# GFNet spectral filter beside an S2-MLP block on one core: spectral chunks in other banks, inverse sums in own buffers, half sums moved, one more unit of seven products

## The chip, the cores and the metric

The kernel runs on one core of one Trainium2 chip. The metric is device time in microseconds (us) of one execution; less is better. The core's engines have queues of their own and meet at semaphores: PE (matrix products, with its weight loads shown as PEld), DVE (vector work), ACT (activations and copies), POOL (more vector work) and SP, whose queue issues the DMAs.

## The reference

The input `x` has 2048 tokens of 448 channels; F is 1792. What is computed, cut to its core:

```
xn = layernorm(x)
A  = irfft2(rfft2(xn) * (w_r + 1j * w_i))          # over tokens and channels
h  = gelu(layernorm(xn) @ w1)                      # 448 x 448
hs = shift(h, quarters by +1, -1, +2, -2 tokens) @ w2
x1 = xn + hs
B  = x1 + gelu(layernorm(x1) @ w3) @ w4            # 448 x 1792, 1792 x 448
out = x + A + B
```

## The kernel before

Every product is made in float16 with each operand split into a high and a low half, so that one product is three passes on the PE (`PASS`: high by high, high by low, low by high). ACT writes the high half of a result from its bank, DVE the low half.

The 2048 tokens are 16 blocks of 128. After the two norms and the products with w1 and w2 (lines L400 to L515) two strands of work run side by side on the PE:

- **The MLP** goes in groups `G` of 256 tokens (0 to 7) and units `fp` of 256 hidden columns (0 to 6). `front(G, fp)` makes 22 matmuls of 256 columns into a bank `pw3` (L400), ACT takes the GELU and the high half `hf`, DVE the low half (L726 to L729). `back(G, fp)` multiplies `hf` by w4 into two banks `acc`: 12 matmuls of 448 columns (L808). `ORD` lists the order of the units in a group.
- **Units of seven products.** For the units in `SEVEN[G]`, `back` runs `seven` instead (L778): the 2 x 2 blocks of a unit (two token blocks, two hidden blocks, w4 cut in two halves of columns) are multiplied in Strassen's manner with seven products in place of eight, so 21 matmuls of 224 columns into `acc` and two banks `side`. `sums` (L736 to L745) makes the sums of the hidden blocks, and `hz`. The sums of w4's blocks must be there before: `w4_sums(j, ...)` loads w4's rows of unit `j` again, makes four sums on DVE (L757) and splits them in a high half on ACT (L280) and a low half on DVE (L281). The sums for units 4, 5 and 0 are made in group 2 (tile `loads`), those for 1, 2 and 3 by `w4_late` at the units that the table `LATE` lists as `(j, G, fp)` (tile `late`).
- **The spectral strand.** After a transform along channels, 16 chunks `c` are worked on by `chunk_a` (`pp` on PE, then `pf` on ACT and DVE, L629 and L630), `chunk_b` (`px` on PE from `pf`, then `te` on ACT and twice on DVE, L644 to L646, and `z` on POOL, L648), `chunk_z` (`zb`, the halves of z, on ACT and DVE, L655 and L656) and `chunk_c` (`pu` on PE from `zb`, then `y` on ACT and DVE, L670 and L671). Each chunk needs its weights `wc` and two constant matrices `gn` by DMA. Then `gather_u` copies the result into `U` (eight DVE copies, L680, for half of the token blocks), `inv_a` makes `pe` on PE (L688), the tile `e` on ACT and DVE (L692 to L699) and `vh`, and `inv_b` makes `py` on PE (L709) and adds it to the output rows `xt`.

PSUM has eight banks, two for each of four tags: `mm`, `tr`, `sp` and `acc`. A new tile of a tag waits until the one two places before it has been read. Before the change `pp` and `pe` are in `tr`; `px`, `pu`, `py` and group 5's `side` are in `sp`. The temporary tiles `te`, `e` and `late` take two places `stage0` and `stage1` in turn.

No order is written out for the engines: a scheduler with a time model of its own merges the strands. MLP fronts and backs are the filler (`FILL`), what empties a bank goes first (`EVAC`), and `behind(key)` holds an instruction back in a queue until the instructions of that key have been placed.

Of the kernel before, what the change touches and what calls it, by code (L numbers as in the profile page):

```python
# [12 lines left out]
F32 = mybir.dt.float32  # L13
# [25 lines left out]
AFTER = [[], [3], [4], [5], [6], [7], [], []]  # L39
EVAC, FILL = 0, 100000  # L40
DH = D // 2
SEVEN = {5: [0, 4, 5], 6: [0, 4, 5, 1, 2, 3], 7: [0, 1, 2, 4, 5]}
ORD = {G: list(range(7)) for G in range(5)} | {5: [1, 2, 3, 6, 0, 4, 5], 6: [0, 4, 5, 1, 2, 3, 6],
                                               7: [0, 1, 2, 4, 5, 3, 6]}

ME = [0, 224] + list(range(2, 224, 2))
# [79 lines left out]
def body(tc, nc, x, wf, w1, w2, w3, w4, c_g, c_n, c_small, out):  # L126
# [14 lines left out]
    def pool(name, bufs=1, side="left", space=None):  # L141
        kw = dict(name=name, bufs=bufs, reuse_waits="tile")
        if space is not None:
            kw["space"] = space
        else:
            kw["side"] = side
        cm = tc.tile_pool(**kw)
        opened[name] = cm
        return cm.__enter__()
# [6 lines left out]
    def bank(tag, name):  # L156
        return ps.tile([128, 512], F32, tag=tag, bufs=2, name=name)

    pc = pool("pc")
    px = pool("px")  # L160
# [16 lines left out]
    def stage(name, n, side, dtype=F32):  # L177
        t = pw.tile([128, 1808], F32, tag=f"stage{side}", bufs=1, name=name)
        return (t if dtype is F32 else t.bitcast(dtype))[:, :n]
# [194 lines left out]
    @contextlib.contextmanager  # L374
    def behind(*key):
        key = key if len(key) > 1 else key[0]
        with contextlib.ExitStack() as st:
            for i in after[key]:
                st.enter_context(tc.issue_after(i))
            yield  # L380
# [202 lines left out]
    def w_scale_end():  # L583
        t = pc.tile([128, 4], F32, name="wt")
        V.tensor_reduce(out=t[:, 0:1], in_=wm, axis=AX.X, op=ALU.max)
        pt = bank("sp", "wpt")
        T.transpose(pt[0:1, 0:128], t[:, 0:1], ident)
        V.tensor_reduce(out=t[0:1, 1:2], in_=pt[0:1, 0:128], axis=AX.X, op=ALU.max)
        V.tensor_scalar(out=t[0:1, 1:2], in0=t[0:1, 1:2], scalar1=2.0 ** -20, scalar2=None, op0=ALU.max)
        pb = bank("sp", "wpb")  # L590
        T.matmul(pb[:, 0:1], ones[0:1], t[0:1, 1:2], start=True, stop=True)
        e = pc.tile([128, 3], I32, name="we")
        V.tensor_copy(out=t[:, 2:3], in_=pb[:, 0:1])
        V.tensor_single_scalar(e[:, 0:1], t.bitcast(I32)[:, 2:3], 0x7F800000, op=ALU.bitwise_and)
        V.tensor_single_scalar(e[:, 1:2], e[:, 0:1], 0x7F800000, op=ALU.bitwise_xor)
        V.tensor_scalar(out=sc[:, 0:1], in0=e.bitcast(F32)[:, 1:2], scalar1=ZPRE, scalar2=None, op0=ALU.mult)
        for h in range(2):
            V.tensor_scalar(out=sc[64 * h:64 * h + 64, 2:3], in0=sc[64 * h:64 * h + 64, 0:1], scalar1=2.0 * h - 1.0,
                            scalar2=None, op0=ALU.mult)
        V.tensor_scalar(out=sc[:, 1:2], in0=e.bitcast(F32)[:, 0:1], scalar1=2.0 ** -21 / (ZPRE * UPRE * VPRE),  # L600
                        scalar2=s12[:, 0:1], op0=ALU.mult, op1=ALU.mult)
        V.tensor_scalar(out=sc[:, 3:4], in0=sc[:, 1:2], scalar1=p12, scalar2=None, op0=ALU.mult)
# [30 lines left out]
    def chunk_b(c):  # L633
        w, k, _ = stream[c]
        pf = pfs.pop(c)
        px_ = bank("sp", f"px{c}")
        for h in range(2):
            for n, (pi, gi) in enumerate(PASS):
                T.matmul(px_[:, DF * h:DF * h + DF], k[:, gi, h], pf[:, pi, h], start=n == 0, stop=n == 2)  # L639
        src = px_[:, :2 * DF]  # L640
        o = stage(f"te{c}", 6 * DF, c % 2)
        e, t = o[:, :2 * DF], o[:, 2 * DF:].rearrange("p (a n) -> p a n", a=2)
        for h in range(2):
            A.activation(out=e[64 * h:64 * h + 64], in_=px_[64 - 64 * h:128 - 64 * h, :2 * DF], func=AF.Copy)  # L644
        V.scalar_tensor_tensor(out=t[:, 0], in0=src, scalar=sc[:, 0:1], in1=w[:, 0], op0=ALU.mult, op1=ALU.mult)
        V.scalar_tensor_tensor(out=t[:, 1], in0=e, scalar=sc[:, 2:3], in1=w[:, 1], op0=ALU.mult, op1=ALU.mult)  # L646
        z = pst.tile([128, 2 * DF], F32, tag="z", bufs=2, name=f"z{c}")
        P.tensor_tensor(out=z, in0=t[:, 0], in1=t[:, 1], op=ALU.add)  # L648
        zs[c] = z
# [8 lines left out]
    def chunk_c(c):  # L658
        _, _, k = stream.pop(c)
        zh = zb[c % 2]  # L660
        pu = bank("sp", f"pu{c}")
        for par in range(2):
            for h in range(2):
                d = pu[:, 256 * par:256 * par + 256].rearrange("p (q k) -> p q k", k=8)[:, :, 4 * h:4 * h + 4]
                for n, (zi, ki) in enumerate(PASS):
                    o = (2 * zi + h) * DF + 113 * par
                    T.matmul(d, zh[:, o:o + 128], k[:, ki, h].rearrange("p (q k) -> p q k", k=4), start=n == 0, stop=n == 2)  # L667
        src = pu[:113].rearrange("p (q n) -> p q n", q=4)
        d = [Y1[:113, p, :, c].rearrange("p q b k -> p q (b k)") for p in range(2)]
        A.activation(out=d[0], in_=src, func=AF.Copy, scale=UPRE)  # L670
        V.scalar_tensor_tensor(out=d[1], in0=src, scalar=UPRE, in1=d[0], op0=ALU.mult, op1=ALU.subtract)  # L671
# [11 lines left out]
    def inv_a(b):  # L683
        pe = bank("tr", f"pe{b}")
        for q in range(4):
            kd = 113 - q // 2
            for n, (ui, ii) in enumerate(PASS):
                T.matmul(pe[:, 113 * q:113 * q + 113], U[b // 8 * 8][ui][:kd, q, b % 8, :],  # L688
                         cI[ii][:kd, 113 * q:113 * q + 113], start=n == 0, stop=n == 2)
        w = stage(f"e{b}", 1126, b % 2)  # L690
        v, e = w[:, 452:900], w[:, 900:1126]
        A.activation(out=e, in_=pe[:, 226:452], func=AF.Copy)  # L692
        u = w[:, 0:452].rearrange("p (a b d) -> p a b d", a=2, b=2)
        uf = w[:, 0:452].rearrange("p (a n) -> p a n", a=2)
        V.tensor_tensor(out=uf[:, 0], in0=pe[:, 0:226], in1=e, op=ALU.add)
        V.tensor_tensor(out=uf[:, 1], in0=pe[:, 0:226], in1=e, op=ALU.subtract)
        va = v.rearrange("p (a d) -> p a d", a=2)
        V.tensor_tensor(out=va[:, :, 0:113], in0=u[:, :, 0], in1=u[:, :, 1], op=ALU.add)
        V.tensor_tensor(out=va[:, ::-1, 223:111:-1], in0=u[:, :, 0, 1:113], in1=u[:, :, 1, 1:113], op=ALU.subtract)  # L699
        vh = pv.tile([128, 2, D], F16, tag="vh", bufs=2, name=f"vh{b}")  # L700
        A.activation(out=vh[:, 0], in_=v, func=AF.Copy, scale=VPRE)
        V.scalar_tensor_tensor(out=vh[:, 1], in0=v, scalar=VPRE, in1=vh[:, 0], op0=ALU.mult, op1=ALU.subtract)
        vhs[b] = vh
# [45 lines left out]
    def w4_sums(j, part):  # L749

        t = part.rearrange("p (k n) -> p k n", n=DH)
        SY.dma_start(t.rearrange("p (f k) n -> p f (k n)", f=2), w4v[:, 2 * j:2 * j + 2])

        def go():
            for o, i, k, op in ((3, 3, 1, ALU.subtract), (1, 1, 0, ALU.subtract),
                                (0, 3, 0, ALU.add), (2, 2, 0, ALU.subtract)):
                V.tensor_tensor(out=t[:, o], in0=t[:, i], in1=t[:, k], op=op)  # L757
            split_w(w4t[j][:, 0], w4t[j][:, 1], t, s4)
        return go
# [60 lines left out]
    def mlp(Gs, hook=None, ahead=1, tags=("mm",)):  # L820
        with prio(FILL):
            todo = [(G, fp) for G in Gs for fp in ORD[G]]
            done = 0
            for n, (G, fp) in enumerate(todo):
                while done < min(n + 1 + (ahead if todo[n] != (7, 5) else 1), len(todo)):
                    front(*todo[done], tags[done % len(tags)])
                    if hook:
                        with prio(EVAC):
                            hook(*todo[done])
                    done += 1  # L830
                back(G, fp)
# [57 lines left out]
    n = 2  # L889
# [148 lines left out]
    close("pfd")  # L1038
    with behind("m", 2, 3):
        w_scale_end()  # L1040
    pst = pool("pst", side="right")
    zb = [pst.tile([128, 4 * DF + 16], F16, name=f"zb{i}") for i in range(2)]
    for i in range(2):
# [10 lines left out]
            chunk_c(i - 3)  # L1054
    close("pst")
    mlp(range(3, 5))
    pv = pool("pv", side="right")
    bs = [*range(8), *range(12, 16), *range(8, 12)]
    for n in range(17):
# [8 lines left out]
                finish(b)  # L1068
    close("pa2")
    pz = pool("pz")  # L1070
    LATE = [(1, 5, 0), (2, 5, 5), (3, 6, 4)]

    def w4_late(G, fp):
        for n, (j, *at) in enumerate(LATE):
# [33 lines left out]
```

## Time and profile before

| | |
|---|---|
| median of 3 runs | 408.02 us (407.68 to 408.14) |
| the profiled execution's own time | 408.05 us |
| its span, first to last instruction | 406.3 us |
| mean granted PE clock | 0.998 |
| PE busy | 399.9 us, 3391 matmuls |
| DVE busy | 333.6 us |
| ACT busy | 255.1 us |
| POOL busy | 100.4 us |

The profile is of one execution. Its page lists each engine's busy time, the span in 40 slices, the DMA queues, the chain of work that ended last, and groups of instructions with count, busy time, mean duration and the idle time ahead of them. Rows of the timeline hold start, duration, engine, line and tile; matmuls are pipelined, so that their pace is read from start to start and not from their durations. Tile names in the profile have no buffer numbers.

### The profile page before, as it was taken

How to read it: one execution, taken by the hardware profiler on the slowest of the kernel's cores; microseconds unless marked ns; L12 is line 12 of the kernel's file. 1: busy time of each engine (PE TensorE's matmuls, PEld its weight loads, DVE VectorE, ACT ScalarE, POOL GpSimd, SP SyncE). 2: the span in 40 equal slices, each digit the busy share in tenths (PEclk: the TensorE clock that was granted, in tenths of full speed). 3: DMA queues.
4: the chain of work that ended last, by engine and by line, in shares of the span. 5: the costliest groups of instructions: out<-in, count | busy, mean ns of one | idle time of the engine just before them, and what ended most of it. 6: DMA issues, size and time to landing. Idle time of an engine off the chain costs nothing.

```text
span 406.3 us, 8732 instructions
## 1 busy us (share of the span) xinstructions
PE 399.9 (98%) x3391; PEld 297.2 (73%) x3391; DVE 333.6 (82%) x702; ACT 255.1 (63%) x433; POOL 100.4 (25%) x158
## 2 busy tenths in 40 slices
PE   8999999999999999999999999999999999999996
PEld 3555555865667877777878878777677779998995
DVE  5898799898947887988698888965999999965645
ACT  4788889874568857655698878853354544353431
POOL 6859910111146946500021111110000000000000
PEclk9999999999999999999999999999999999999999
DMA  8978975567489661637256556510011023100101
GB/s 280 389 272 160 249 152 138 122 121 163 95 225 266 234 191 46 219 95 185 72 144 164 162 142 161 139 27 2 24 69 70 24 90 92 47 2 2 45 2 45
DMA packets 54596, 52.07 MB, mean 128 GB/s; under 512 B 35678, under 2 KB 48542, under 8 KB 54556
## 3 DMA queue, kind: packets, MB, share of 16 engines
q1 hardware_dynamic: 54556, 51.53, 46.0%
q8 instruction: 26, 0.43, 0.4%
q14 instruction: 14, 0.11, 0.1%
HBM read 38.28 MB, written 3.67 MB: 103 GB/s over the span
## 4 chain that ended last, share of the span: by engine, by line
PE 87%; POOL 5%; DMA 2%; DVE 2%; ACT 2%; issue 1%; SPq 0%; POOLq 0%; ACTq 0%
PE pw L400 33%; PE acc L808 23%; PE pw L478 6%; PE side L778 4%; PE acc L778 3%; PE pu L667 3%; PE ps L567 3%; PE pe L688 2%; PE pp L622 2%; PE px L639 2%; PE py L709 2%; PE pw L420 2%; DMA w1s<-w 1%; POOL xt L336 1%; DMA h<-x2mem 1%
## 5 line engine op out<-in xcount | busy, mean ns | idle before, releaser
L400 PE MATMUL pw<-x2mem,w3p 128*128 128x256 f16 x1232 | 151.3, 273 | 0.0
L400 PEld LDWEIGHTS <-w3p 128*128 128x128 f16 x1232 | 118.9, 98 | 19.3
L808 PE MATMUL acc<-w4p,hf 128*128 128x448 f16 (+1 forms) x516 | 104.4, 348 | 0.0
L808 PEld LDWEIGHTS <-hf 128*128 128x128 f16 x516 | 50.1, 98 | 37.6
L726 ACT ACTIVATE pw<-pw,pe 128x512 f32<-128x512 f32 x42 | 27.4, 654 | 26.8 <-PE pw L400 26.6
L729 DVE SCALAR_TENSOR_TENSOR hf<-pw,h,hf 128x512 f16<-128x512 f32 x42 | 31.3, 746 | 12.9 <-ACT hf L728 12.7
L478 PE MATMUL pw<-w2p,h 128*128 128x448 f16 x176 | 35.8, 353 | 0.9 <-DMA h<-x2mem 0.9
L420 PE MATMUL pw<-w1p,xT 128*128 128x448 f16 x176 | 34.9, 352 | 0.1
L648 POOL TENSOR_TENSOR z<-te 128x450 f32<-128x450 f32 x16 | 15.7, 983 | 70.8 <-DVE te L646 65.9
L728 ACT ACTIVATE hf<-pw,h 128x512 f16<-128x512 f32 x42 | 28.9, 687 | 5.0 <-PE acc L808 4.0
L478 PEld LDWEIGHTS <-h 128*128 128x128 f16 x176 | 17.0, 98 | 17.0 <-DMA h<-x2mem 2.0
L744 ACT ACTIVATE hz<-g,h 128x896 f16<-128x896 f32 x14 | 14.6, 1044 | 23.1 <-DVE g L741 23.1
L420 PEld LDWEIGHTS <-xT 128*128 128x128 f16 x176 | 17.1, 99 | 16.1 <-DVE xT L394 0.4
L778 PEld LDWEIGHTS <-hz 128*128 128x128 f16 x294 | 28.3, 98 | 0.6
L629 ACT ACTIVATE pf<-pp 64x450 f16<-64x450 f32 x32 | 17.4, 544 | 12.5 <-DVE pf L630 9.7
L630 DVE TENSOR_TENSOR pf<-pp,pf 64x450 f16<-64x450 f32 x32 | 19.9, 622 | 5.1 <-ACT pf L629 4.7
L745 DVE SCALAR_TENSOR_TENSOR hz<-g,h,hz 128x896 f16<-128x896 f32 x14 | 16.1, 1148 | 6.8 <-ACT hz L744 6.8
L550 POOL TENSOR_TENSOR f<-xr 128x452 f32<-128x452 f32 x16 | 19.7, 1251 | 0.6
L558 DVE TENSOR_TENSOR xh<-f,xh 128x452 f16<-128x452 f32 x16 | 14.3, 916 | 5.7 <-ACT xh L557 5.7
L644 ACT ACTIVATE te<-px 64x450 f32<-64x450 f32 x32 | 17.3, 541 | 1.2 <-PE px L639 0.6
L738 ACT ACTIVATE g<-pw,pe 128x512 f32<-128x512 f32 x14 | 9.6, 683 | 11.3 <-PE pw L400 11.3
L547 POOL TENSOR_TENSOR xr<-xf 128x452 f32<-128x452 f32 x8 | 9.2, 1156 | 22.3 <-issue 16.4
(188 smaller groups left out, 705.7 us busy)
## 6 DMA issues: line engine op xcount, KB each, us to landing
wc<-wf SPq DMA_DIRECT2D x32, 225.0 KB, 3.7
wl<-wf SPq DMA_DIRECT2D x8, 450.0 KB, 4.3
xt<-x SPq DMA_DIRECT2D x8, 448.0 KB, 7.1
xf<-x SPq DMA_DIRECT2D x8, 448.0 KB, 4.6
loads<-x SPq DMA_DIRECT2D x7, 448.0 KB, 4.0
out<-xt SPq DMA_DIRECT2D x13, 224.0 KB, 1.9
w3raw<-w SPq DMA_DIRECT2D x3, 896.0 KB, 10.8
gn<-c_g SPq DMA_DIRECT2D x16, 128.0 KB, 3.0
```

Source lines behind the costliest of these rows:

```text
L400: T.matmul(ps_out, wp[:, wi + t, cols], xT[:, xi + t, tok], start=t == 0 and wi + xi == 0, stop=t == 3 and wi == 4)
L420: m = T.matmul(pm[:, :D], xTs[g][:, xi + t, 128 * i:128 * i + 128], w1p[:, wi + t], start=t == 0 and p == 0, stop=t == 3 and p == 2)
L478: T.matmul(pm[:, :D], h[:, k], w2p[:, w], start=n == 0, stop=n == 10)
L550: P.tensor_tensor(out=f[:, :, k:k + 2].rearrange("p b s d -> p s b d"), in0=u[:, :, 0], in1=u[:, :, 1], op=op)
L629: A.activation(out=hi, in_=src, func=AF.Copy)
L630: V.tensor_tensor(out=lo, in0=src, in1=hi, op=ALU.subtract)
L644: A.activation(out=e[64 * h:64 * h + 64], in_=px_[64 - 64 * h:128 - 64 * h, :2 * DF], func=AF.Copy)
L726: A.activation(out=pm, in_=pm, func=AF.Gelu_apprx_tanh, scale=r3)
L728: i = A.activation(out=h[:, 0], in_=pm, func=AF.Copy, scale=h3)
L729: j = V.scalar_tensor_tensor(out=h[:, 1], in0=pm, scalar=h3, in1=h[:, 0], op0=ALU.mult, op1=ALU.subtract)
L778: m = T.matmul(to, h[:, hi, 128 * blk:128 * blk + 128], b[wi], start=new and n == 0, stop=n == 2 and (last if blk in (2, 5, 3, 0) else end ...
L808: m = T.matmul(to, h[:, hi, o:o + 128], w4p[0][:, wi, f, r], start=first and f % 2 == 0 and n == 0, stop=end and f % 2 == 1 and n == 2, sk ...
```

## The change

1. `px` and `pu` of chunks 14 and 15 take banks of the tag `tr` instead of `sp`.
2. The tile `e` of `inv_a` gets three buffers of its own in the pool `pv`.
3. The half sums of w4 for units 1 and 2 are made in group 4, behind units 0 and 2, from two tiles `early` of a new pool; `LATE` holds only unit 3, now at group 6's first unit.
4. Unit 1 of group 5 becomes a fourth unit of seven products there, and is the group's last in `ORD`.

```diff
-SEVEN = {5: [0, 4, 5], 6: [0, 4, 5, 1, 2, 3], 7: [0, 1, 2, 4, 5]}
-ORD = {G: list(range(7)) for G in range(5)} | {5: [1, 2, 3, 6, 0, 4, 5], 6: [0, 4, 5, 1, 2, 3, 6],
+SEVEN = {5: [0, 4, 5, 1], 6: [0, 4, 5, 1, 2, 3], 7: [0, 1, 2, 4, 5]}
+ORD = {G: list(range(7)) for G in range(5)} | {5: [2, 3, 6, 0, 4, 5, 1], 6: [0, 4, 5, 1, 2, 3, 6],
...
-        px_ = bank("sp", f"px{c}")
+        px_ = bank("tr" if c in (14,15,) else "sp", f"px{c}")
...
-        pu = bank("sp", f"pu{c}")
+        pu = bank("tr" if c in (14,15,) else "sp", f"pu{c}")
...
-        w = stage(f"e{b}", 1126, b % 2)
+        w = pv.tile([128, 1126], F32, tag="e", bufs=3, name=f"e{b}")
...
+    pt = pool("pt")
     pst = pool("pst", side="right")
...
     mlp(range(3, 5))
+    for n, j in enumerate((1,2,)):
+        with behind(("f", 4, 2 * n + 0)):
+            w4_sums(j, pt.tile([128, 896], F32, tag="early", bufs=2, name=f"early{j}"))()
+    close("pt")
     pv = pool("pv", side="right")
...
-    LATE = [(1, 5, 0), (2, 5, 5), (3, 6, 4)]
+    LATE = [(3,6,0)]
```

The order of instructions changes from the last chunks on. The first place is on the DVE, after the low half of group 4's first unit (`hf40`); `pf15` is what px15 reads, `pu10` and `px13` are banks of chunks 10 and 13. Before:

```order
L630 TENSOR_TENSOR pf14_3285<-pp14_3272,pf14_3285 64x2x225
L656 TENSOR_TENSOR zb0_2540<-z12_3248,zb0_2540 128x450
L671 SCALAR_TENSOR_TENSOR y1_1548<-pu10_3250,y1_1548 113x4x128
L645 SCALAR_TENSOR_TENSOR te13_3299<-px13_3292,sc_138,wc13_3209 128x450
L646 SCALAR_TENSOR_TENSOR te13_3299<-te13_3299,sc_138,wc13_3209 128x450
L630 TENSOR_TENSOR pf15_3341<-pp15_3328,pf15_3341 64x450
L729 SCALAR_TENSOR_TENSOR hf41_3769<-pw3_41_3745,h3_666,hf41_3769 128x512
L630 TENSOR_TENSOR pf15_3341<-pp15_3328,pf15_3341 64x2x225
```

After, at the same place:

```order
L757 TENSOR_TENSOR early1_3998<-early1_3998 128x224
L630 TENSOR_TENSOR pf14_3288<-pp14_3275,pf14_3288 64x2x225
L656 TENSOR_TENSOR zb0_2543<-z12_3251,zb0_2543 128x450
L671 SCALAR_TENSOR_TENSOR y1_1548<-pu10_3253,y1_1548 113x4x128
L757 TENSOR_TENSOR early1_3998<-early1_3998 128x224
L645 SCALAR_TENSOR_TENSOR te13_3302<-px13_3295,sc_138,wc13_3212 128x450
L646 SCALAR_TENSOR_TENSOR te13_3302<-te13_3302,sc_138,wc13_3212 128x450
L630 TENSOR_TENSOR pf15_3344<-pp15_3331,pf15_3344 64x450
L757 TENSOR_TENSOR early1_3998<-early1_3998 128x224
L729 SCALAR_TENSOR_TENSOR hf41_3772<-pw3_41_3748,h3_666,hf41_3772 128x512
L757 TENSOR_TENSOR early1_3998<-early1_3998 128x224
L630 TENSOR_TENSOR pf15_3344<-pp15_3331,pf15_3344 64x2x225
```

The four sums of early1 stand among the same instructions, all four ahead of the second part of pf15. Behind it follow, after the change, the two te of chunk 14, the low half of early1, zb of chunk 13, y of chunks 11 and 12 and zb of chunk 14.

The second place is on the PE, from px14 to the w4 unit of `hf41`; equal matmuls that follow each other, and weight loads, are left out. Before, px14 comes after 7 matmuls of pw3_42 and the 12 of pu11, and then:

```order
L639 MATMUL px14_3348<-pf14_3285,gn0_14_3268 128x225
...
L400 MATMUL pw3_42_3786<-x2mem_119,w3p_132 128x256
...
L808 MATMUL acc40_3772<-w4p_991,hf41_3769 128x448
...
L400 MATMUL pw3_43_3825<-x2mem_119,w3p_132 128x256
...
L667 MATMUL pu12_3362<-gn1_12_3158,zb0_2540 128x32x4
...
L639 MATMUL px15_3379<-pf15_3341,gn0_15_3324 128x225
```

After, px14 is the first thing behind the w4 unit of `hf40`:

```order
L639 MATMUL px14_3351<-pf14_3288,gn0_14_3271 128x225
...
L400 MATMUL pw3_42_3789<-x2mem_119,w3p_132 128x256
...
L667 MATMUL pu11_3309<-gn1_11_3105,zb1_2544 128x32x4
...
L667 MATMUL pu12_3365<-gn1_12_3161,zb0_2543 128x32x4
...
L639 MATMUL px15_3382<-pf15_3344,gn0_15_3327 128x225
...
L808 MATMUL acc40_3775<-w4p_991,hf41_3772 128x448
```

px15 has moved ahead of the w4 unit of `hf41` (12 matmuls): between px14 and px15 there are now 3 matmuls of pw3_42, 12 of pu11, 12 of pu12 and 14 of pw3_42, and behind px15 5 of pw3_42 and that unit. Then come 7 of pw3_43, 2 of pu14, 12 of pu13 and 10 of pu14, 15 of pw3_43, a w4 unit, and pu15 among the matmuls of pw3_44. The first `pe` has 7 matmuls of pw3_45 ahead of it where it had 2 of pw3_46 before.

The third place is SP's queue, as the difference; `y_1300` to `y_1407` are rows for the MLP's input, `early` and `late` w4's rows, `gn_15` the last chunk's second constant:

```order
 L514 DMA_TRANSPOSE x2mem<-y_1300 128x7x128 x2
 L514 DMA_TRANSPOSE x2mem<-y_1303 128x7x128 x2
+L752 DMA early_3998<-w 128x2x448
+L752 DMA early_4006<-w 128x2x448
 L514 DMA_TRANSPOSE x2mem<-y_1404 128x7x128 x2
 L514 DMA_TRANSPOSE x2mem<-y_1407 128x7x128 x2
...
+L614 DMA gn_14_3273<-c_n 128x512
+L752 DMA late_4852<-w 128x2x448
+L614 DMA gn_15_3329<-c_n 128x512
```

The two early loads have moved up to the MLP's input transposes of the second stage, and late3 stands ahead of the last load of a chunk, where three late loads stood among the output's DMAs.

## The prediction

> **What bounds the kernel now.** I read the page's first part, then the waits of the PE, then the chain that ended last and the PE's rows in order of time.
>
> ```profile
> span 406.3 us, 8732 instructions
> PE 399.9 (98%) x3391; PEld 297.2 (73%) x3391; DVE 333.6 (82%) x702; ACT 255.1 (63%) x433; POOL 100.4 (25%) x158
> PE wps L838 <- DVE wsrc L192: 1.2, 1, 1.2
> PE pw L478 <- DMA h<-x2mem: 0.9, 3, 0.4
> PE pta L389 <- POOL xt L336: 0.7, 1, 0.7
> PE pm L260 <- DVE pt L258: 0.4, 1, 0.4
> 347.62 1.15 PE side L778 x12
> 374.10 2.27 PE acc L808 x12
> 376.37 2.40 PE pw L400 x22
> ```
>
> The PE is busy 98% of the span. Its four listed waits sum to 3.2 us, and all stand at lines of the first, second and norm stages, which the change does not touch. From the first GELU product on, the PE goes from matmul to matmul. The last three rows give the pace: 2.27/12 = 189 ns for 448 columns, 1.15/12 = 96 ns for 224, 2.40/22 = 109 ns for 256. So the time is the sum of PE work plus whatever new wait appears, and an edit can gain only by taking columns off the PE.
>
> ```profile
> 257.00 2.43 PE L808 MATMUL acc<-w4p,hf 128*128 128x448 f16 x12
> 259.27 0.93 PE L400 MATMUL pw<-x2mem,w3p 128*128 128x256 f16 x7
> 260.03 0.83 PE L667 MATMUL pu<-gn,zb 128*128 128x128 f16 x12
> 260.70 0.74 PE L639 MATMUL px<-pf,gn 128*128 128x225 f16 x6
> 261.28 1.80 PE L400 MATMUL pw<-x2mem,w3p 128*128 128x256 f16 x15
> ...
> 266.40 0.74 PE L639 MATMUL px<-pf,gn 128*128 128x225 f16 x6
> ...
> 257.00:270.00 13.00, 13.00 (x113) 9.75 (x111) 10.69 (x17) 10.49 (x19) 1.96 (x2) 1.00 0.35 93
> 270.00:285.00 15.00, 15.00 (x147) 11.62 (x146) 7.93 (x18) 5.97 (x11) 0.98 (x1) 1.00 0.04 10
> 285.00:340.00 55.00, 55.00 (x511) 41.79 (x509) 53.10 (x125) 25.56 (x49) 0.00 (x0) 1.00 0.17 60
> ```
>
> From start to start, 12 pu matmuls take 0.67 us (56 ns each) and 6 px matmuls 0.58 us (97 ns each). In the stage rows (length, then busy PE, PEld, DVE, ACT, POOL), the DVE is free for 2.3 us of 13, then 7.1 us of 15, and then almost never: 53.1 of 55 us during the inverse transform. The PE is full in all three.
>
> **The change, part by part.** *Seven products for unit 1 of group 5.* Twelve matmuls of 448 columns go (12 x 189 = 2.27 us) and 21 of 224 come (21 x 96 = 2.02 us): **-0.25 us** on the PE, which is on the path.
>
> A rule of the Trainium skill speaks against this term: its page "TensorE: Matmul & The Clock Gate", section "Back-to-back issue gap", gives about 81 ns per matmul at 128 columns and 131 ns at 512 for a stream of weight loads and matmuls. On a straight line between these an estimate is 123 ns at 448 and 93 ns at 224, so twelve become 1.47 us, 21 become 1.96 us, and the term would be +0.49 us. The rows above (189 and 96 ns) do not agree with it, and the measurement decides.
>
> ```profile
> L745 DVE SCALAR_TENSOR_TENSOR hz<-g,h,hz 128x896 f16<-128x896 f32 x14 | 16.1, 1148 | 6.8 <-ACT hz L744 6.8
> L741 DVE TENSOR_TENSOR g<-g 128x384 f32<-128x384 f32 x14 | 7.8, 555 | 0.2
> L740 DVE TENSOR_TENSOR g<-g 128x256 f32<-128x256 f32 x14 | 5.9, 421 | 5.4 <-ACT g L738 5.4
> L729 DVE SCALAR_TENSOR_TENSOR hf<-pw,h,hf 128x512 f16<-128x512 f32 x14 | 10.5, 747 | 5.4 <-ACT hf L728 5.4
> L757 DVE TENSOR_TENSOR late<-late 128x224 f32<-128x224 f32 x12 | 4.7, 390 | 0.6 <-DMA late<-w 0.4
> L281 DVE SCALAR_TENSOR_TENSOR x2mem<-late,pe,x2mem 128x896 f16<-128x896 f32 x3 | 3.4, 1146 | 0.0
> L280 ACT ACTIVATE x2mem<-late,pe 128x896 f16<-128x896 f32 x3 | 3.1, 1028 | 0.0
> 340.00:360.00 20.00, 20.00 (x197) 18.86 (x196) 18.84 (x33) 9.10 (x11) 0.00 (x0) 1.00 0.14 47
> ```
>
> On the DVE the seven-product unit costs 421 + 555 + 1148 - 747 ns = 1.38 us more. It stands where two sets of half sums stood, each 4 x 390 + 1146 ns = 2.7 us, and these have gone from there, so the DVE is lighter by 5.4 - 1.4 = 4.0 us in the stretch to 360 us. I cost it at nothing. The set for unit 3 moves ahead by some units inside group 6, into that freed time: nothing.
>
> *The half sums for units 1 and 2 in group 4.* The same 5.4 us of DVE and 2 x 1028 ns of ACT now stand from 257 us on, ahead of spectral work that the PE reads. The windows have 9.4 us of free DVE time between 257 and 285 us, but not evenly spread.
>
> *Banks.* Chunks 14 and 15 take the first product's banks. In the new order the PE reaches px14 right after the first w4 unit of group 4, and px15 after px14, 3 pw, 24 pu and 14 pw matmuls. From the start of the second row above that is 259.27 + 0.58 + 0.33 + 1.34 + 1.53 = **263.05 us**, where before px15 starts at 266.40. px15 needs the second half of pf15.
>
> ```profile
> 256.99 0.63 DVE L630 TENSOR_TENSOR pf<-pp,pf 64x450 f16<-64x450 f32 x1
> 257.66 0.63 DVE L656 TENSOR_TENSOR zb<-z,zb 128x450 f16<-128x450 f32 x1
> 258.32 0.69 DVE L671 SCALAR_TENSOR_TENSOR y<-pu,y 113x512 f16<-113x512 f32 x1
> 258.93 0.68 DVE L645 SCALAR_TENSOR_TENSOR te<-px,sc,wc 128x450 f32<-128x450 f32 x1
> 259.52 0.68 DVE L646 SCALAR_TENSOR_TENSOR te<-te,sc,wc 128x450 f32<-128x450 f32 x1
> 261.42 0.63 DVE L630 TENSOR_TENSOR pf<-pp,pf 64x450 f16<-64x450 f32 x1
> 263.71 0.69 DVE L645 SCALAR_TENSOR_TENSOR te<-px,sc,wc 128x450 f32<-128x450 f32 x1 [0.28 <-ACT te L644]
> 279.23 2.77 DVE L680 COPY U<-y 113x1024 f16<-113x1024 f16 x8
> 282.68 0.36 PE L688 MATMUL pe<-csm,U 113*128 113x113 f16 x4
> ```
>
> The second pf15 ends at 262.05 us. The four subtractions and additions on early1 stand ahead of it now. The te rows show that the next instruction starts 0.09 us before the last ends, so four cost between 4 x 0.30 = 1.2 and 4 x 0.39 = 1.56 us, and pf15 ends between 263.25 and 263.61. The PE waits 0.2 to 0.56 us; I take **+0.35**, the value nearer to a running queue. Behind that wait on the PE's queue stand the rest of pw3_42 and the w4 unit, so all of it is paid.
>
> Next is pu14. After pf15 (263.4) the DVE has two te (0.6 each), the early1 low half (1.06), a zb and two y (0.6 each) and then zb of chunk 14: it ends at about 268.1. The PE, from px15 at 263.4, has 6 px, 5 pw, 12 w4, 7 pw, 2 and 12 pu matmuls: 263.4 + 0.58 + 0.55 + 2.27 + 0.76 + 0.11 + 0.67 = 268.3. That is covered by 0.2 us: taken at nothing, bounded by 0.5.
>
> Then the U copies. Ahead of pe0 the PE now has one w4 unit (2.27 us) and 17 pw matmuls (1.85) less, so it arrives at 282.68 - 4.1 + 0.35 = 278.9 us. The DVE's list from 256.99 to the last copy is 8 sums x 0.30, 2 low halves x 1.06, 19 operations of pf, zb, y and te x 0.6, three hf x 0.66 (0.75 less the overlap) and the copies, 2.77: 2.4 + 2.1 + 11.4 + 2.0 + 2.8 = 20.7 us, ending at 277.7 if it never waits, against the PE's need at 278.9 (first halves) to 279.3 (second halves). I expect about 0.7 us of waits on ACT and POOL in it, so no stall, bounded by 1.5 us.
>
> From there DVE and PE both run the inverse stage about 4 us sooner, with one hf (0.75 us) less on the DVE; its 1.9 free us of 55 leave room for small waits. I add **+0.1** there, between 0 and 0.8.
>
> *Own e buffers.* Three buffers in place of two shared ones take away waits of ACT and DVE only; the PE waited for none of them: nothing.
>
> *Loads.*
>
> ```profile
> 92.54 5.42 SPq L514 DMA_TRANSPOSE x2mem<-y  x4
> 104.78 5.24 SPq L514 DMA_TRANSPOSE x2mem<-y  x4
> late<-w SPq DMA_DIRECT2D x3, 448.0 KB, 3.5
> 265.13 0.98 POOL L648 TENSOR_TENSOR z<-te 128x450 f32<-128x450 f32 x1 [3.81 <-DVE te L646]
> gn<-c_n SPq DMA_DIRECT2D x16, 128.0 KB, 3.3
> ```
>
> The two early loads are issued between the transposes at 92.5 and 104.8, where SP has nothing from 97.96 on; their wait is for a matmul of the first product, which the h transposes ahead of them on SP need as well. With 3.5 us to landing they are in by about 103: nothing. late3 now stands on SP ahead of the last c_n load and waits for z14, which ends near 266 us; that load waits anyway for pu13, at about 268.3. Landing 3.3 us later it is in at 271.7, and pu15 comes 15 pw, 12 w4 and one pw after pu14, at about 272.8: covered by 1.1 us.
>
> **Sum.** -0.25 + 0.35 + 0.1 = +0.2 us on the profiled execution's 408.05 us (span 406.3 and 1.75 around it). The median of the runs, 408.02, is 0.03 below that, so both give **408.2 us**. About 0.2%, 0.8 us, is what a measurement of this kernel can tell from no change.
>
> **Rivals.**
> 1. *All waits are covered.* If the four sums slip into gaps, or pf15 is done by 263.05, only the PE term is left: 407.8 us. For it: the PE has no wait in these stages now. Against: the DVE is gapless from 256.99 to 263.4 in the rows. Chance 0.20.
> 2. *Slower: the DVE becomes the bound ahead of the inverse stage.* The copies of U end after the PE gets to pe0. The stall begins once the DVE's waits between 257 and 278 us sum to about 1.4 us, and it decides from about 2.0 on. For it: such waits are there now (0.28 us ahead of te alone), and the early low halves wait for ACT, with zb and y queued behind. Against: the list itself needs only 20.7 us. With 2.5 to 3.3 us of waits pe0 stalls 1.1 to 1.9 us; with the other terms that gives 409.3 to 410.1, in the middle 409.7. Chance 0.21.
> 3. *The seven products do not shorten the PE's work.* By the page's spacing the term is +0.49 in place of -0.25, so 408.9 us. The rows for 224 and 448 columns speak against it. Chance 0.01.
> 4. *Faster by over 0.8 us.* The change takes 0.25 us off the PE and no stage has a PE wait to give back, so this needs something that the profile does not show. Time 407.0. Chance 0.04.
>
> **How the numbers follow.** The forecast (stalls of 0.1 to 0.95 us in all, 407.9 to 408.7) gets 0.54. Same is 0.54 + 0.20 = 0.74, slower 0.21 + 0.01 = 0.22, faster 0.04. The range goes from 407.6 (rival 1 less 0.2 us, about half the spread of the runs, 407.68 to 408.14) to 409.5, which leaves out the faster case and about half of rival 2.
>
> **What would show it.** In the profile after: PE rows with 21 matmuls of L778 more and 12 of L808 fewer; a wait of px on the DVE's pf of 0.2 to 0.6 us near 263 us; pe starting near 278.9 us; no PE wait on U, te or vh over 0.3 us. A PE wait on U copies of 1 us or more, or several on vh in the inverse stage, makes it wrong towards rival 2; no PE wait at all makes it rival 1.

## The result, and the profile after

The changed kernel takes 409.06 us (median of 9 runs, 408.86 to 409.34), the kernel before 408.02 (9 runs, 407.62 to 408.38). The ratio is 1.0028 (95%: 1.0018 to 1.0038): slower by 0.28%, 1.04 us. That lies inside the range, but above the band of the forecast (407.9 to 408.7) and below that of rival 2 (409.3 to 410.1). "Same" had 0.74, and by the 0.8 us that the prediction set for it, it was not the same.

The first part of the page, two of the waits of the PE, and the PE's group of w4 products, of the kernel after:

```profile
span 407.3 us, 8758 instructions
PE 400.3 (98%) x3400; PEld 298.2 (73%) x3400; DVE 336.2 (83%) x704; ACT 255.4 (63%) x433; POOL 100.6 (25%) x158
PE px L639 <- DVE pf L630: 0.8, 1, 0.8
PE pu L667 <- DVE zb L656: 0.2, 1, 0.2
L808 PE MATMUL acc<-w4p,hf 128*128 128x448 f16 (+1 forms) x504 | 102.0, 348 | 0.0
```

The PE has 9 matmuls more (21 - 12), and two waits that it did not have. To see the change apart from the stages ahead of it, whose waits differ from run to run, I use the *products' part*: from the start of the first matmul of L808 to the end of the PE's last row. In the PE's timeline of the kernel before it is 401.32 + 1.69 - 87.39 = 315.62 us:

```profile
87.39 0.54 PE L808 MATMUL acc<-w4p,hf 128*128 128x448 f16 x2
401.32 1.69 PE L808 MATMUL acc<-w4p,hf 128*128 128x448 f16 x14
```

and in that of the kernel after 401.26 + 2.73 - 87.33 = 316.66 us, so all of the 1.04 us is in it:

```profile
87.33 0.54 PE L808 MATMUL acc<-w4p,hf 128*128 128x448 f16 x2
...
261.74 1.36 PE L400 MATMUL pw<-x2mem,w3p 128*128 128x256 f16 x11
263.86 0.74 PE L639 MATMUL px<-pf,gn 128*128 128x225 f16 x6 [0.75 <-DVE pf L630]
...
268.01 0.94 PE L667 MATMUL pu<-gn,zb 128*128 128x128 f16 x14
269.20 0.73 PE L667 MATMUL pu<-gn,zb 128*128 128x128 f16 x10 [0.24 <-DVE zb L656]
...
279.02 0.93 PE L400 MATMUL pw<-x2mem,w3p 128*128 128x256 f16 x7
279.78 0.36 PE L688 MATMUL pe<-csm,U 113*128 113x113 f16 x4
401.26 2.73 PE L808 MATMUL acc<-w4p,hf 128*128 128x224 f16 x21
```

Read from start to start, as in the prediction: 11 matmuls of 109 ns from 261.74 bring the PE to px15 at 262.94, and it starts at 263.86, 0.92 us late. 14 of 56 ns from 268.01 bring it to the rest of pu14 at 268.79, and it starts at 269.20, 0.41 us late. (The bracket and the waits list give less, since a row's modelled end runs past the next start.) I call such lateness a *loss*. -0.25 + 0.92 + 0.41 = +1.08 us, against +1.04 measured. The first pe comes 7 x 109 ns after 279.02, without a loss.

What delayed pf15 and zb of chunk 14 stands in the timelines of POOL and of the DVE:

```profile
260.83 1.01 POOL L648 TENSOR_TENSOR z<-te 128x450 f32<-128x450 f32 x1 [5.22 <-DVE te L646]
265.17 1.76 POOL L648 TENSOR_TENSOR z<-te 128x450 f32<-128x450 f32 x1 [3.33 <-ACT y L670]
```

```profile
260.61 0.61 DVE L630 TENSOR_TENSOR pf<-pp,pf 64x450 f16<-64x450 f32 x1
261.14 0.95 DVE L757 TENSOR_TENSOR early<-early 128x224 f32<-128x224 f32 x1
262.01 0.73 DVE L729 SCALAR_TENSOR_TENSOR hf<-pw,h,hf 128x512 f16<-128x512 f32 x1
262.68 0.37 DVE L757 TENSOR_TENSOR early<-early 128x224 f32<-128x224 f32 x1
263.08 0.63 DVE L630 TENSOR_TENSOR pf<-pp,pf 64x450 f16<-64x450 f32 x1
...
264.94 1.15 DVE L281 SCALAR_TENSOR_TENSOR x2mem<-early,pe,x2mem 128x896 f16<-128x896 f32 x1
266.00 1.41 DVE L656 TENSOR_TENSOR zb<-z,zb 128x450 f16<-128x450 f32 x1
268.53 0.61 DVE L656 TENSOR_TENSOR zb<-z,zb 128x450 f16<-128x450 f32 x1
```

The third sum of early1 takes 0.95 us where the fourth takes 0.37, and it ends at 262.09, 0.25 us after POOL's add of z13 (261.84). zb of chunk 13 takes 1.41 us where that of chunk 14 takes 0.61, and ends at 267.41, 0.48 us after POOL's add of z14 (266.93). That add itself took 1.76 us in place of 0.98: it began while the DVE's low half of early1 ran, and ended 0.84 us after it. The long DVE rows and POOL's add read all their inputs from SBUF. The sum costs 0.57 us on the way to px15, zb 0.78 on the way to pu14.

My theory: the two losses are the DVE's queue ahead of pf15, as forecast, plus a mutual blocking of the DVE and POOL (each holds the other up while it reads SBUF), which was not forecast. The rivals: the queue's length alone; the early sums as such, wherever the PE stands; the banks alone.

### The profile page after: what moved, and what is told of

It reads as the page before. It is cut to its first block, busy times and chain, and to the rows that moved or that the text cites. A ratio compares the mean times of both kernels' runs of the same rounds, so it can differ in the third digit from the quotient of the medians.

```text
span 407.3 us, 8758 instructions
## 1 busy us (share of the span) xinstructions
PE 400.3 (98%) x3400; PEld 298.2 (73%) x3400; DVE 336.2 (83%) x704; ACT 255.4 (63%) x433; POOL 100.6 (25%) x158
## 4 chain that ended last, share of the span: by engine, by line
PE 83%; DVE 5%; POOL 5%; ACT 3%; issue 2%; DMA 1%; DVEq 0%; POOLq 0%
PE pw L400 31%; PE acc L808 21%; PE pw L478 6%; PE side L778 4%; PE acc L778 3%; PE ps L567 3%; PE pe L688 2%; PE py L709 2%; PE wps L838 2%; PE pp L622 2%; PE pw L420 2%; PE pu L667 2%; PE px L639 2%; POOL xt L336 1%; DMA h<-x2mem 1%
## 5 line engine op out<-in xcount | busy, mean ns | idle before, releaser
L808 PE MATMUL acc<-w4p,hf 128*128 128x448 f16 (+1 forms) x504 | 102.0, 348 | 0.0
L808 PEld LDWEIGHTS <-hf 128*128 128x128 f16 x504 | 48.9, 98 | 36.6
L729 DVE SCALAR_TENSOR_TENSOR hf<-pw,h,hf 128x512 f16<-128x512 f32 x41 | 30.4, 743 | 11.8 <-ACT hf L728 11.4
L778 PEld LDWEIGHTS <-hz 128*128 128x128 f16 x315 | 30.3, 98 | 0.9
L744 ACT ACTIVATE hz<-g,h 128x896 f16<-128x896 f32 x15 | 15.6, 1040 | 17.3 <-DVE g L741 14.1
L745 DVE SCALAR_TENSOR_TENSOR hz<-g,h,hz 128x896 f16<-128x896 f32 x15 | 17.2, 1148 | 10.1 <-ACT hz L744 10.0
```

The lines of the kernel that those rows point to most:

```text
L729: j = V.scalar_tensor_tensor(out=h[:, 1], in0=pm, scalar=h3, in1=h[:, 0], op0=ALU.mult, op1=ALU.subtract)
L778: m = T.matmul(to, h[:, hi, 128 * blk:128 * blk + 128], b[wi], start=new and n == 0, stop=n == 2 and (last if blk in (2, 5, 3, 0) else end ...
L808: m = T.matmul(to, h[:, hi, o:o + 128], w4p[0][:, wi, f, r], start=first and f % 2 == 0 and n == 0, stop=end and f % 2 == 1 and n == 2, sk ...
```

## Experiments

Each kernel ran beside the kernel before on its chip, whose median there was 408.07 to 408.23 us. Losses are from the PE's timeline.

| kernel | median us | ratio to before (95%) | products' part against before, us | losses of the PE after 120 us |
|---|---|---|---|---|
| after, again | 409.24 | 1.0024 (1.0015 to 1.0033) | +1.06 | 0.92 px15, 0.41 pu14 |
| fourth unit alone | 409.65 | 1.0028 (1.0015 to 1.0040) | +0.07 | 0.30 near 346 |
| fourth unit, own e | 408.94 (one run) | | +0.08 | 0.30 near 346 |
| after, early sums late | 408.78 | 1.0011 (1.0002 to 1.0020) | +0.61 | 0.90 px15 |
| after, old banks | 409.03 | 1.0022 (1.0014 to 1.0031) | +0.46 | 0.59 pu14, 0.13 pu12 |
| after, short z adds | 408.33 | 1.0011 (1.0001 to 1.0022) | +0.10 | 0.35 px15 |
| after, POOL adds | 410.43 (one run) | | +2.17 | as after, and 1.03 at 307 |
| after, POOL fills | 409.16 (one run) | | +1.09 | as after |
| one early set | 408.29 | 1.0005 (0.9996 to 1.0014) | -0.25 | none |
| fifth unit, one early set | 410.18 | 1.0051 (1.0038 to 1.0063) | +1.72 | 1.64 at 336 to 339, 0.55 at 342 to 343 |
| fifth unit, two early sets | 408.99 | 1.0018 (1.0009 to 1.0027) | +0.40 | 0.37 at 338, 0.56 at 342 to 343 |
| the same, four hz | 407.65 | 0.9986 (0.9976 to 0.9997) | -0.47 | none |

The medians hold more than the change. The fourth unit alone ran from 407.98 to 411.33 us in 12 runs; the profiled one was the fastest, with a span of 406.2 us, and the others had spans of 407.0 to 409.6. The kernel with the old banks spent 2.2 us outside its span where the kernel before spent 1.75. Where this time goes no timeline shows, and both stay open. I judge the theories by the products' part, which is read from one execution of each kernel.

**The kernel after, again**, for comparison on the same chip.

> The kernel after, unchanged, for comparison on the same chip: 409.1 us, with the wait of px15 at 0.9 us and that of pu14 at 0.4.

Both losses came back to 0.01 us.

**The fourth unit alone.**

```diff
 # on the kernel before
-SEVEN = {5: [0, 4, 5], ...
+SEVEN = {5: [0, 4, 5, 1], ...
-... 5: [1, 2, 3, 6, 0, 4, 5], ...
+... 5: [2, 3, 6, 0, 4, 5, 1], ...
```

> The kernel before with the fourth unit of seven products alone (SEVEN and ORD of group 5 changed; banks, e tile and half sums as before, the sums for unit 1 still late). Theory: 12 x 189 ns go from the PE and 21 x 96 ns come, -0.25 us, and no new wait, so 407.8 us. Rival: seven products do not shorten the PE's work, or the DVE's 1.4 us more per unit comes back as a wait: 408.3 us or more.

There is no loss between 120 and 340 us, but 0.30 us near 346, between the matmuls of two units of seven products; with it the -0.25 became +0.07. The forecast of 407.8 was wrong by that loss, and the median by more, for a reason that stays open.

**The fourth unit with the own e buffers.**

```diff
 # on the fourth unit alone
-        w = stage(f"e{b}", 1126, b % 2)
+        w = pv.tile([128, 1126], F32, tag="e", bufs=3, name=f"e{b}")
```

> The fourth unit of seven products and the own e buffers, with banks and half sums as before. In the kernel with the fourth unit alone the PE lost 0.33 us between 340 and 350 us, where the DVE had waited 1.3 us for a late load whose place the e tiles share. Theory: with own e buffers the late loads come earlier, the two late sets do not bunch up at 338 to 345 us, and that loss goes: products' part 0.25 us below before. Rival (the two late sets and the fourth unit are too much for the DVE there): 0.3 us or more are lost again.

The two late sets now stand apart, as the theory said (their low halves on the DVE from 330.54 and from 341.85 us, where they followed each other from 343.18), but 0.30 us are lost again. What stands ahead of the hz on ACT is another thing in each kernel. With the fourth unit alone it is the two late high halves (342.10 to 344.08 us), and hz follows without a gap. With the own e buffers ACT stands idle, until a matmul of the PE releases one of the three buffers of hz, which are used in turn:

```profile
343.98 1.98 ACT L744 ACTIVATE hz<-g,h 128x896 f16<-128x896 f32 x2 [2.17 <-PE side L778]
```

So the own e buffers took one wait away, and what the PE lost stayed the same.

**After, with the half sums late as before** (banks, e buffers and the fourth unit kept).

```diff
 # on the kernel after
-    for n, j in enumerate((1,2,)):
-        with behind(("f", 4, 2 * n + 0)):
-            w4_sums(j, pt.tile(...early...))()
-    LATE = [(3,6,0)]
+    LATE = [(1, 5, 0), (2, 5, 5), (3, 6, 4)]
```

> The kernel after without the early half sums: they are made late, as before; banks, e buffers and the fourth unit stay. The PE then comes to px15 another 1.75 us sooner (at about 261.2 us), while pf15's second half ends at 262.05 as in the kernel before. Theory (the banks pull px15 ahead of pf15, with or without the sums): px15 waits about 0.85 us, and pe0 up to 0.5 us on the U copies: 408.6 to 409.1 us. Rival (the early sums are the cause): no such wait, 407.8 us.

The PE's row of px15 and the DVE's row of what it waits for:

```profile
262.39 0.74 PE L639 MATMUL px<-pf,gn 128*128 128x225 f16 x6 [0.73 <-DVE pf L630]
261.61 0.63 DVE L630 TENSOR_TENSOR pf<-pp,pf 64x450 f16<-64x450 f32 x1
```

px15 loses 0.90 us without a single early sum: the banks let the PE's order run ahead of pf15. pu14 loses nothing, and neither does pe0, which it reaches at 276.99. The early sums alone are not the cause.

**After, with the old banks.**

```diff
 # on the kernel after
-        px_ = bank("tr" if c in (14,15,) else "sp", f"px{c}")
+        px_ = bank("sp", f"px{c}")
-        pu = bank("tr" if c in (14,15,) else "sp", f"pu{c}")
+        pu = bank("sp", f"pu{c}")
```

> The kernel after with px and pu of chunks 14 and 15 back in the sp banks; early sums, e buffers and the fourth unit stay. The PE then reaches px15 some 4.2 us later than in the kernel after, long past pf15. Theory: the stretched DVE sums are still there beside POOL's z adds, but nothing waits for them; PE without a wait on pf or zb, 407.8 us. Rival: the early sums cost time wherever the PE stands, because DVE and POOL are slowed: 408.6 to 409.1 us.

px15 loses nothing, as the theory said, but pu14 loses 0.59 us, which neither side had. The PE's row and three of the DVE's:

```profile
274.09 0.83 PE L667 MATMUL pu<-gn,zb 128*128 128x128 f16 x12 [0.43 <-DVE te L645]
269.04 2.08 DVE L757 TENSOR_TENSOR early<-early 128x224 f32<-128x224 f32 x4
272.22 1.15 DVE L281 SCALAR_TENSOR_TENSOR x2mem<-early,pe,x2mem 128x896 f16<-128x896 f32 x1
273.35 0.69 DVE L645 SCALAR_TENSOR_TENSOR te<-px,sc,wc 128x450 f32<-128x450 f32 x1
```

pu14 needs the bank that te of chunk 15 empties, and the sums and the low half of early2 stand ahead of that te (the four sums in 2.08 us; POOL's add of z14 runs beside the first). So the banks of the change do take away a wait that its early sums bring, and bring one of their own.

**After, with short z adds.**

```diff
 # on the kernel after
+        if c in (13, 14, 15):
+            P.memset(z, 0.0)
+            P.tensor_tensor(out=z[:, 0:8], in0=t[:, 0, 0:8], in1=t[:, 1, 0:8], op=ALU.add)
+        else:
             P.tensor_tensor(out=z, in0=t[:, 0], in1=t[:, 1], op=ALU.add)
```

> The kernel after in which POOL adds only 8 of the 450 columns of z for chunks 13, 14 and 15 and fills the rest with zeros ahead of time (that part of the sum is left out). DVE and PE have the same queues up to px15. Theory (DVE with two SBUF inputs and POOL's add block each other): the early1 sum that took 0.95 us takes 0.38 and zb of chunk 13 that took 1.41 takes 0.63, the wait of px15 falls from 0.91 to about 0.35 us and that of pu14 goes: 408.1 us. Rival (the length of the DVE queue alone): px15 still late by 0.9 us, about 409.0 us.

The same rows as of the kernel after: px15 on the PE, then the third sum, the low half and zb of chunk 13 on the DVE, then the short adds of z13 and z14 on POOL.

```profile
264.72 0.74 PE L639 MATMUL px<-pf,gn 128*128 128x225 f16 x6 [0.19 <-DVE pf L630]
262.57 0.37 DVE L761 TENSOR_TENSOR early<-early 128x224 f32<-128x224 f32 x1
265.80 1.15 DVE L281 SCALAR_TENSOR_TENSOR x2mem<-early,pe,x2mem 128x896 f16<-128x896 f32 x1
266.86 0.63 DVE L660 TENSOR_TENSOR zb<-z,zb 128x450 f16<-128x450 f32 x1
262.26 0.23 POOL L650 TENSOR_TENSOR z<-te 128x8 f32<-128x8 f32 x1 [1.83 <-DVE te L646]
266.03 0.98 POOL L650 TENSOR_TENSOR z<-te 128x8 f32<-128x8 f32 x1 [3.54 <-DVE te L646]
```

This kernel leaves out 442 of the 450 columns of z for three chunks. The sum is back at 0.37 us and zb at 0.63; px15 loses 0.35 us and pu14 nothing: the theory's numbers. (zb of chunk 14 no longer waits for a long add either. In the kernel after that wait was not the last: ACT had the high half of that zb done at 267.54 us, and the DVE came to it only at 268.53.) The second short add is the blocking seen from the other side: 0.23 us alone, 0.98 beside the low half, and it ends 0.06 us after that (266.95).

**After, with 16 POOL adds in the inverse stage**, and with 16 fills.

```diff
 # on the kernel after, in inv_a
-        w = pv.tile([128, 1126], ...
+        w = pv.tile([128, 1578], ...
         A.activation(out=e, in_=pe[:, 226:452], func=AF.Copy)
+        je = e.unsqueeze(1).to_broadcast([128, 2, 226])
+        P.tensor_tensor(out=w[:, 1126:1578]..., in0=je, in1=je, op=ALU.add)
 # or, in place of the last two lines
+        P.memset(w[:, 1126:1578], 0.0)
```

> The kernel after with one more POOL add (e to itself, 452 columns, both inputs in SBUF, its result unused) for each of the 16 blocks of the inverse transform, where POOL had nothing and the DVE is full. It starts when ACT has written e. Theory (mutual blocking): DVE rows with a PSUM input stay as they are (e<-pe,e 0.38 us, xt<-py 0.68), while rows with both inputs in SBUF (e<-e 0.38, vh<-e,vh 0.61) that meet an add wait for its end: 0.3 to 1.0 us each, 5 to 16 us over the stage, and the kernel, whose DVE has 2 us of 55 free there, comes out 3 to 13 us slower than 409.1. POOL's adds show times well over 0.98 us where they were held. Rival (no blocking; the long rows of the kernel after have another cause): all these means unchanged and 409 us.

> The same with POOL fills of 452 columns with a constant in place of the 16 adds: they write SBUF and read nothing from it. Theory (what blocks is POOL's read): DVE rows unchanged and 409.1 us. Rival (any POOL instruction blocks, or POOL's write does): rows with both inputs in SBUF longer, in proportion to the fills' time.

With the adds, two rows of POOL and four of the DVE beside them:

```profile
281.72 1.84 POOL L694 TENSOR_TENSOR e<-e 128x452 f32<-128x452 f32 x2 [10.01 <-ACT e L692]
290.84 2.72 POOL L694 TENSOR_TENSOR e<-e 128x452 f32<-128x452 f32 x2 [1.78 <-ACT e L692]
...
282.29 0.38 DVE L697 TENSOR_TENSOR e<-pe,e 128x226 f32<-128x226 f32 x1
282.59 0.38 DVE L698 TENSOR_TENSOR e<-pe,e 128x226 f32<-128x226 f32 x1
282.89 1.23 DVE L700 TENSOR_TENSOR e<-e 128x226 f32<-128x226 f32 x2
...
291.40 1.36 DVE L527 SCALAR_TENSOR_TENSOR xr<-xt,s,xr 128x448 f32<-128x448 f32 x1
```

The rows with a PSUM input run at their 0.38 us in the middle of an add (281.72 to 283.56). The next one, with both inputs in SBUF, and its second together take 1.23 us, where two rows of the next line took 0.68 right behind them. The row of xr, 0.68 us when alone at 289.96, takes 1.36 beside the second pair of adds, and the pair 2.72 us in place of 1.84. The kind of the effect was as the theory said, its size was not: the rows that were held took some 3.1 us more in all, not 5 to 16, and the kernel lost 1.1 us against the kernel after in the products' part, not 3 to 13, in one loss of 1.03 us at 307 where the PE waited for an hf. ACT's e releases the add just ahead of the two DVE rows with a PSUM input, and the greater part of 12 of the 16 adds stood beside rows of that kind. Ahead of that hf on the DVE's queue, two copies of U were held as well, which have one input, in SBUF. Beside adds they took 1.65 us, where the last two took 0.75:

```profile
298.94 1.65 DVE L680 COPY U<-y 113x1024 f16<-113x1024 f16 x2
302.99 0.75 DVE L680 COPY U<-y 113x1024 f16<-113x1024 f16 x2
```

The first group of e<-e rows between 285 and 335 us, of the kernel after, with the adds, and with the fills:

```profile
L698 DVE TENSOR_TENSOR e<-e 128x226 f32<-128x226 f32 x14 | 5.3, 385 | 0.1
L700 DVE TENSOR_TENSOR e<-e 128x226 f32<-128x226 f32 x14 | 5.9, 426 | 0.1
L699 DVE TENSOR_TENSOR e<-e 128x226 f32<-128x226 f32 x14 | 5.4, 390 | 0.1
```

The fills, shorter (0.48 us) and at other times, cost nothing (+1.09 us where the kernel after has +1.04 and +1.06). A fill did not hold a row that began while it ran, as a row of xr with both inputs in SBUF shows; but a fill that met two copies of U (301.01 to 301.77) took 0.97 us itself:

```profile
291.05 0.48 POOL L693 MEMSET e<- 128x452 f32 x1 [4.24 <-DVE vh L703]
291.15 0.68 DVE L527 SCALAR_TENSOR_TENSOR xr<-xt,s,xr 128x448 f32<-128x448 f32 x1
301.22 0.97 POOL L693 MEMSET e<- 128x452 f32 x1 [3.26 <-DVE vh L703]
```

So what held the DVE's rows is POOL's reading.

**One early set.** Only unit 1's half sums early, behind a unit later; banks as before.

```diff
 # on the kernel with the old banks
-    for n, j in enumerate((1,2,)):
-        with behind(("f", 4, 2 * n + 0)):
+    for j, fp_ in [(1, 1)]:
+        with behind(("f", 4, fp_)):
             w4_sums(j, pt.tile(...early...))()
-    LATE = [(3,6,0)]
+    LATE = [(2, 5, 5), (3, 6, 4)]
```

> Banks as before; own e buffers; only unit 1's half sums early, behind unit 1 of group 4 and so behind the first te of chunk 13; units 2 and 3 late at (5, 5) and (6, 4); the fourth unit of seven products in group 5. Theory: px15 comes at about 266.3 us, past pf15; te of chunk 15, for whose bank pu14 waited in the kernel without the bank change, has only one set of sums ahead of it; so no wait of the PE after 120 us, and the products' part falls by 0.25 us against before: 407.8 us. Rival (early sums always cost a wait): 0.3 to 0.6 us of new waits between 260 and 280 us, 408.1 to 408.4.

No loss, and the products' part is 0.25 us below that of before: the term of the fourth unit, by itself. The time can't be told from before's (1.0005, 0.9996 to 1.0014).

**A fifth unit of seven products.** First with that one early set, then with two (behind units 1 and 3 of group 4), then with the same and a fourth buffer of hz.

```diff
 # on the kernel with one early set
-SEVEN = {5: [0, 4, 5, 1], ...           ORD 5: [2, 3, 6, 0, 4, 5, 1]
+SEVEN = {5: [0, 4, 5, 1, 2], ...        ORD 5: [3, 6, 0, 4, 5, 1, 2]
 # second
-    for j, fp_ in [(1, 1)]:             LATE = [(2, 5, 5), (3, 6, 4)]
+    for j, fp_ in [(1, 1), (2, 3)]:     LATE = [(3, 6, 4)]
 # third
-        h = pz.tile([128, 2, 7 * 128], F16, tag="hz", bufs=3, ...
+        h = pz.tile([128, 2, 7 * 128], F16, tag="hz", bufs=4, ...
```

> As the kernel with one early set of sums, and unit 2 of group 5 a fifth unit of seven products there. Theory: another 12 x 189 ns go and 21 x 96 ns come, so -0.5 us against before; the DVE has by 360 us the same work as before (one set of 2.7 us less, two seven-product units of 1.38 more): 407.5 us. Rival (the DVE's sums for the units come late): waits on hz between 335 and 365 us of 0.3 us or more, 407.8 or more.

> Banks as before; own e buffers; the half sums of units 1 and 2 both early, but behind units 1 and 3 of group 4, so that the second te of chunk 15 stands ahead of the second set; unit 3's late at (6, 4); units 1 and 2 of group 5 as fourth and fifth unit of seven products. Theory: te of chunk 15 is done before the PE needs its bank, zb of chunk 15 ends near 274.5 us where pu15 comes at 277; and no late set stands beside the two more units, so the DVE has 2.7 us less to do by 360 us than in the kernel before: no new wait after 120 us, twice -0.25: 407.5 us, 1.55 below the kernel after. Rival (the DVE bound returns, as in the kernel with the fifth unit and one early set): waits on vh, xt or hz of 0.5 us or more between 330 and 350 us, 408 us or more.

The first fell to its rival: vh waits behind a late set on the DVE from 336 us on. In the second that is gone, but 0.37 us are lost at 338 and 0.56 at 342 to 343. The PE's row at 343 and the one of ACT that it comes from:

```profile
343.01 0.27 PE L778 MATMUL side<-w4p,hz 128*128 128x224 f16 x1 [0.25 <-DVE hz L745]
340.73 1.98 ACT L744 ACTIVATE hz<-g,h 128x896 f16<-128x896 f32 x2 [3.99 <-PE side L778]
```

ACT stood idle for 3.99 us until a matmul of the PE released an hz. (The expectation that follows counts the products' part to the start of the last matmul, 0.26 us less for every kernel: 315.37 for before, and 314.90 came out.)

> The kernel with two early sets (behind units 1 and 3) and the fifth unit, with four buffers of hz in place of three. There the PE lost 0.37 us at 338.2 and 0.41 at 343.0: at 343 it waited for an hz that ACT could begin only when the PE had released one of three buffers. Theory (the ring of hz is what the fifth unit runs into): the loss at 343 goes, that at 338 (a side bank still held by the last block's output) stays, the products' part is 315.2 to 315.3 us and the time 407.9. Rival (the chain from GELU to hz is too long in itself): both losses stay, 315.8 and 408.4 or more.

Both losses went, the one at 338 too, which I had expected to stay. Of the waits of the PE only those ahead of the products are left:

```profile
PE wps L838 <- DVE wsrc L192: 1.2, 1, 1.2
PE pta L389 <- POOL xt L336: 0.6, 1, 0.6
PE pw L478 <- DMA h<-x2mem: 0.4, 1, 0.4
PE pw L478 <- DVE xt L479: 0.3, 1, 0.3
```

This kernel, 407.65 us (407.32 to 408.36), is faster than before by 0.14% (0.9976 to 0.9997) and so than the kernel after, and its products' part is 0.47 us below before's, where two times -0.25 were due. That the same ring of buffers made the loss at 346 in the kernel with the own e buffers is likely, but was not tried; with the fourth unit alone ACT's late high halves stood last ahead of it.

## Why the prediction was right or wrong

- **The PE term, -0.25:** right. It stands alone in the kernel with one early set, and nearly doubled with five units. Rival 3's +0.49 did not come.
- **px15, +0.35:** wrong in size; it was 0.92. The PE's arrival was right (263.05 forecast, 262.94 read), pf15's end was not: 263.71 against 263.25 to 263.61. I had sized the four sums at 0.30 to 0.39 us each, from a row of 12 late sums beside which POOL stands still. One of them met POOL's z add and took 0.95. Without the long adds the loss is 0.35 us, the forecast's own value; but 0.15 of it is the way from pf15's end to px15's start (263.71 to 263.86 in the kernel after, and 264.57 to 264.72 here), which I had not counted, so that the equal number is in part luck.
- **pu14, covered by 0.2, bounded by 0.5:** not covered; 0.41 was lost, inside the bound. zb of chunk 14 ended at 269.14, not at 268.1, mostly by the 0.78 us that zb of chunk 13 ahead of it took longer.
- **The cause on the PE's side** was named rightly as the banks: with the old ones px15 loses nothing, with the new ones 0.90 us even without early sums. That the old banks with these early sums cost a wait of their own (te of chunk 15, 0.59) was not seen.
- **U copies and the inverse stage, 0 and +0.1:** no loss there. pe0 came at 279.78 in place of 278.9, since px15 started 0.46 us after its forecast (263.86 against 263.4) and pu14 lost 0.41. The copies of U ended at 279.86, not at 277.7: three rows held by POOL's adds, the two above and the first sum of early2 (270.92, 0.79 us), are 1.76 us of that. Rival 2 had the right sign, and its times begin 0.24 us above the result, but not the place: the DVE did not end late before pe0. Rival 1, all covered, needed px15 without a loss.
- **Own e buffers, early loads, the late3 load:** nothing, as said. **The seven's work on the DVE, nothing:** so in the kernel after, yet the fourth unit without early sums loses 0.30 us at 346.

The step that failed is thus the price of a DVE instruction taken from a row with idle POOL; the forecast of "same" hung on it, since 0.35 + 0.57 + 0.41 us less 0.25 is over the 0.8 us that a measurement can tell. That the time still lies inside the range is luck: the range was stretched to 409.5 for rival 2, whose mechanism did not come.

The profile before could have warned of it. One DVE instruction of an earlier stage, with both inputs in SBUF, stands there 16 times with one shape, and with these shortest, median and longest times in ns:

```profile
L558 DVE TENSOR_TENSOR xh<-f,xh x16: 611/761/1482, 122.1 to 174.3; 128x452 f16<-128x452 f32 x16
```

Its eight rows beside which POOL stands still take 0.61 to 0.63 us, its eight rows beside POOL's adds 0.89 to 1.48.

## What to carry to other kernels

Before a vector instruction that reads SBUF alone is moved, look at what POOL runs at its new place, and price the overlap at up to the other's whole instruction, in both directions. A mean hides this: ask for the shortest and the longest time of one shape, and see what ran beside the long ones. An order that brings the busiest engine sooner to a step spends the cover of that step's inputs; cover of a few tenths of a microsecond, on a queue without gaps, is none. When a change bundles several edits, read each from the part of the trace it touches: here 1.3 us of new waits hid a true gain of 0.25.

## What the runs showed of the hardware

The DVE and POOL stop each other when both read SBUF on all inputs: the DVE's 0.38 us sum took 0.95 and its 0.63 us zb 1.41, each ending 0.25 and 0.48 us after POOL's add; POOL's 0.98 us add took 1.76, and an add of 8 columns 0.98 in place of 0.23, beside the DVE's low half. DVE rows with one input in PSUM kept their 0.38 us beside an add, and fills by POOL left the DVE's rows as they were (0.68 us for xr). Copies of U, with their one input in SBUF, were held by adds too (1.65 us for two, 0.75 alone), and held a fill (0.97 us, 0.48 alone). In the trace this is no wait: the held instruction only reads as long. The Trainium skill's page "SBUF — State Buffer", section "Who interferes with whom", states that a DVE instruction with two SBUF inputs contends with a GpSimd (POOL) instruction that reads SBUF, not with one that only writes it, and that the order of issue decides which of the two blocks. The sum, zb and xr agree with the first part, and the second add of 8 columns, which the low half held, with the second.
